# Fused attention and two expert layers on one core: weight staging in eight tiles, expert 1's token rows loaded beside expert 0's, and a PSUM pool of its own for the attention scores

## Chip, cores and metric

The kernel runs on one core of one Trainium2 chip. The metric is device time in microseconds; three runs of the kernel before have a median of 816.23 us (815.91 to 817.96).

## What is computed

Attention with hash buckets feeds a dense feed-forward layer, and that feeds a mixture of eight experts in which every token goes to its best two. The last part is the one that matters here:

```python
top2 = np.argpartition(-noisy_logits, 2, axis=1)[:, :2]
...
for e in range(E):                       # E = 8 experts
    for k in range(2):
        mask = top2[:, k] == e
        h = np.maximum(x[mask] @ w1[e], 0.0)          # 512 -> 1024
        out[mask] += top2_w[mask, k, None] * (h @ w2[e])   # 1024 -> 512
```

There are 1536 tokens of 512 numbers. Every product is made of three fp16 products of high and low parts, so most tiles exist twice (high, low).

## The kernel before, in words

The program has two parts. In the first, a loop over steps `g` (up to 96 attention tiles, `NU` = 96, and a tail of 20 more steps) interleaves attention, the dense layer and the router. Functions are put on a step by `at(g, f, ...)`, and the program is written out in that order; from step 100 on the order on every engine is exactly the written one. In the second part, a list `seq` holds the experts' matrix products, one entry a step `x`: `l1(e, p, f)` makes one block of 128 of the hidden layer for the tokens of part `p` of expert `e`, and `l2(e, p, t)` makes the output of 128 tokens. Experts 1 to 7 have one part of 400 token slots. Expert 0 has two parts, slots 0 to 255 (0,0) and 256 to 399 (0,1), so that its first part can start before the last tokens are routed.

**Order of `seq`.** Eight `l1` of (0,0), its two `l2`; eight `l1` of (0,1), its two `l2`; then expert 1 and so on. The `hold` line puts the first `l1` of the next expert ahead of the `l2` of the last one. At step `x` the program issues first the evictions of step `x-1` (`l1_out` on ACT, L842, then DVE, L843; `l2_out` on ACT, L873, or on ACT and DVE for the short last tile), then the products of step `x`, then what `at` put there.

**Tokens.** The router (`route`) ends for each block of tokens in two scatters to DRAM (`slots`, POOL, L718). `e_load(e, p)` reads an expert's slots back with one transposing DMA to the tile `xg` (L789) and reads the few numbers of weight and address per token to the tile `mt` by small DMAs (L794, L799; where the slots are not a multiple of 128, DVE first writes a default, L797). `e_meta` turns `mt` into weights and addresses on DVE (L809 to L819). `xg` and `mt` have two buffers each. The last block of tokens, chunk (5,1), is routed by the generator `gen` while the `l1` of (0,0) run; its steps are drawn `QX` at a time from step `QS` = 3 on and finished at step `QE`. PE takes part with the transposes `xp` (L578), the logits `pz` (L611, L613) and the running count `pp` (L684, L685), which needs the mask `mk` (DVE, L667).

**Weights.** An expert's weights come in eight blocks of 128 x 1024 fp32 (0 to 3 of `w1`, 4 to 7 of `w2`). `w12_load` brings a block to a staging tile `w32` (L761, L764, on SP's queue), and `w12_split` makes its high part on ACT (L775) and its low part on DVE (L776). There are four staging tiles, so block 4 can be loaded only when block 0 is split.

**Queues.** All of this part's loads are issued by SP, in written order; an entry that waits holds everything behind it. The scatters and the output additions (L880) are issued by POOL.

**PSUM.** Of eight banks, the pool `psr` has one, the pool `psum` seven during attention (two score tiles `s` of two banks, two of tag `h`, one `pv`). When the first part is over, `psum` is closed and `psum2` takes its seven banks: three `ph` for `l1`, three `py` for `l2`, one `xp`. A first tile in a bank of `psum2` waits for the last reader of what lay there. The code behind `tc.If(most > CAP)` (an expert with over 400 tokens) is not entered with these inputs.

Of the kernel before, what the change touches and what calls it, by code (L numbers as in the profile page):

```python
# [8 lines left out]
F32 = mybir.dt.float32  # L9
# [10 lines left out]
DM = H * D  # L20
# [37 lines left out]
PARAM.update(KA={(0, 0, 0): -15, (0, 0, 1): -6, (0, 1, 0): -5, (0, 1, 1): -4, (0, 2, 0): -1, (0, 2, 1): 1, (0, 3, 0): 4, (0, 3, 1): 5, (1, 0, 0): 37, (1, 0, 1): 39, (1, 1, 0): 44, (1, 1, 1): 46, (1, 2, 0): 42, (1, 2, 1): 51, (1, 3, 0): 47, (1, 3, 1): 51}, QA={(0, 0, 0): -15, (0, 0, 1): -3, (0, 0, 2): 1, (0, 0, 3): 3, (0, 1, 0): 8, (0, 1, 1): 9, (0, 1, 2): 17, (0, 1, 3): 21, (0, 2, 0): 24, (0, 2, 1): 28, (0, 2, 2): 30, (0, 2, 3): 33, (1, 0, 0): 37, (1, 0, 1): 41, (1, 0, 2): 47, (1, 0, 3): 52, (1, 1, 0): 57, (1, 1, 1): 56, (1, 1, 2): 60, (1, 1, 3): 69, (1, 2, 0): 72, (1, 2, 1): 69, (1, 2, 2): 80, (1, 2, 3): 84}, VA={(0, 0, 0): -1, (0, 0, 1): -3, (0, 1, 0): -1, (0, 1, 1): -1, (0, 2, 0): 0, (0, 2, 1): 0, (0, 3, 0): -1, (0, 3, 1): -2, (1, 0, 0): -1, (1, 0, 1): -1, (1, 1, 0): 2, (1, 1, 1): -4, (1, 2, 0): -3, (1, 2, 1): -3, (1, 3, 0): 2, (1, 3, 1): -2}, PV={(0, 0, 0): 4, (0, 0, 1): 5, (0, 0, 2): 6, (0, 0, 3): 5, (0, 1, 0): 6, (0, 1, 1): 4, (0, 1, 2): 4, (0, 1, 3): 5, (0, 2, 0): 5, (0, 2, 1): 5, (0, 2, 2): 5, (0, 2, 3): 6, (1, 0, 0): 4, (1, 0, 1): 5, (1, 0, 2): 4, (1, 0, 3): 5, (1, 1, 0): 5, (1, 1, 1): 5, (1, 1, 2): 5, (1, 1, 3): 6, (1, 2, 0): 6, (1, 2, 1): 4, (1, 2, 2): 4, (1, 2, 3): 4}, RA={0: 18, 1: 18, 2: 19, 3: 24, 4: 18}, W=[(g,1) for g in [-6, -4, -3, -1, 0, 0, 1, 1, 2, 4, 4, 7, 8, 8, 9, 10, 11, 12, 13, 14, 15, 16, 16, 17, 18, 20, 20, 22, 22, 23, 23, 24]], EC=lambda g:'AA', LE=lambda nc:nc.sync, HI=lambda g:'AAAA'[g%4], LO=lambda g:[0, 0, 0, 1, 0, 0, 0, 1][g%8]==1, S1=[8, 8, 8, 8, 8, 11, 13, 22], ST={0: 4, 1: 4, 2: 5, 3: 4, 4: 5, 5: 3}, NG=28, WS=lambda i:'PAAA'[i%4], HE=lambda nm,b:'DPDD'[2*(nm=='k')+b], OE=lambda nm,b:'DTDD'[2*(nm=='k')+b], SC=lambda nm,b:'DADD'[2*(nm=='k')+b], R1=2, I0=26, IS=1, O0=56, OS=1, GM=100, BK=3, OH=3, QX=10, QS=3, QE=7, VF=0, T0=12, T1=17, EL=10, WX=5, WL=2, PC=2, GW=2, E0=8, WB=2)  # L58
# [3 lines left out]
def fused(ctx: ExitStack, tc: tile.TileContext, q, k, v, proj, w_in, w_out, w_gate, w_noise, noise,  # L62
# [10 lines left out]
    psum_ctx = ExitStack()  # L73
    psum = psum_ctx.enter_context(tc.tile_pool(name="psum", bufs=2, space=bass.MemoryType.PSUM))
# [173 lines left out]
    def qk(g):  # L248
        b, cc, hp, h, t = where(g)
        qt, kt = qts[b, hp, cc], kts[b, hp]  # L250
        ps = psum.tile([128, 1024], F32, name="s")
# [335 lines left out]
    def route(ci, ta=0, tb=CT):  # L587
# [153 lines left out]
    def r_counts():  # L741
        pc = psum2.tile([128, E], F32, name="pc", tag="py")
# [103 lines left out]
    def l2(e, p, t):  # L846
        py = psum2.tile([128, DM], F32, name="py", bufs=3)
# [132 lines left out]
    for ci in range(B * NCH):  # L980
# [9 lines left out]
        if ci == B * NCH - 2:  # L990
# [63 lines left out]
    psum_ctx.close()  # L1054
# [19 lines left out]
    for e in range(1, E):  # L1074
# [35 lines left out]
    with tc.If(most > CAP):  # L1110
        with tc.tile_pool(name="ov", bufs=1) as ov:
# [8 lines left out]
            hto = ov.tile([128, FE // 128, 2, 128], F16)  # L1120
            yo = ov.tile([128, DM], F32)
            x = ov.tile([128, 1024], F32)
            wt = [wts.tile([128, 2, 4096], F16, name=f"wo{i}", tag="w") for i in range(2)]
            nc.vector.memset(cur, 0.0)
            with tc.For_i(0, E, 1) as e:
# [5 lines left out]
                with tc.If(here > CAP):  # L1131
# [12 lines left out]
                    with tc.For_i(0, (OV + 127) // 128, 1) as k_:  # L1144
                        with tc.If(here > k_ * 128 + CAP):
# [33 lines left out]
                            py = psum2.tile([128, DM], F32, name="pyo", tag="py", bufs=3)  # L1179
# [37 lines left out]
```

## Time and profile before

| what | value |
|---|---|
| median of three runs | 816.23 us (815.91 to 817.96) |
| the profiled execution's own time | 815.95 us |
| its span in the trace | 814.2 us |
| busy share of the span | PE 87%, DVE 66%, ACT 55%, POOL 33% |

The span is what the trace shows from first to last instruction; 1.75 us of the execution's time lie around it. Busy shares are averages: the first 440 us or so (attention) and the experts from 574 us on have different limits, and the stretch between them is where one part hands over to the other.

### The profile page before, as it was taken

Reading aid. Unit: us, or ns where it says so; the run is one execution under the profiler, and the core shown is the slowest. Engines: PE = TensorE matmul, PEld = TensorE weight load, DVE = VectorE, ACT = ScalarE, POOL = GpSimd, SP = SyncE. Lnnn points to the kernel's source line nnn. Section 1 sums busy time; section 2 is a strip of 40 time slices with the busy share of each in tenths; the row PEclk is TensorE's granted clock in tenths of the full one; section 3 lists DMA queues with packets and bytes.
Section 4 is the critical chain, followed back from the end, with each engine's and each line's share of the span. In section 5 each row is a group of like instructions: output and inputs, shape, how many; then the busy total and the mean of one; then the engine's idle time right before and its main releaser. Section 6 shows DMA issues by size and latency. Waiting matters only on the chain.

```text
span 814.2 us, 14902 instructions
## 1 busy us (share of the span) xinstructions
PE 705.3 (87%) x5408; PEld 434.8 (53%) x5409; DVE 541.1 (66%) x1368; ACT 446.9 (55%) x866; POOL 268.0 (33%) x305
## 2 busy tenths in 40 slices
PE   1676578988988798888999999887999999999995
PEld 1343346645754575467567666454545545555452
DVE  8998699996897789569779626673635436354320
ACT  3778768765876586467557525342534435344220
POOL 6444646560444054304212233221121211302113
PEclk9878779999999999999999999998999999999998
DMA  8999689999999999996696650949668768577313
GB/s 219 219 254 218 163 182 195 255 265 237 175 167 211 154 194 194 220 175 106 103 197 115 98 182 17 277 125 196 142 186 226 159 177 198 139 203 156 79 18 44
DMA packets 266942, 139.20 MB, mean 171 GB/s; under 512 B 224176, under 2 KB 242672, under 8 KB 266864
## 3 DMA queue, kind: packets, MB, share of 16 engines
q1 hardware_dynamic: 260848, 125.04, 69.1%
q0 software_dynamic: 6016, 13.16, 8.9%
q8 instruction: 43, 0.70, 0.4%
q14 instruction: 35, 0.29, 0.1%
HBM read 61.48 MB, written 23.20 MB: 104 GB/s over the span
## 4 chain that ended last, share of the span: by engine, by line
PE 43%; DVE 6%; DMA 3%; ACT 2%; issue 1%; POOL 0%; POOLq 0%; ACTq 0%; DVEq 0%
PE ph L832 15%; PE py L863 15%; PE px L472 7%; PE h L461 2%; DMA xg<-slots 2%; DVE er L324 1%; PE py L857 1%; PE pv L369 1%; DMA et<-er 1%; DVE th L491 1%; PE s L255 1%; ACT er L315 1%; DVE e L267 1%; DMA qt<-qsa 0%; POOL out_dram L880 0%
## 5 line engine op out<-in xcount | busy, mean ns | idle before, releaser
L461 PE MATMUL h<-xt,wi 128*128 128x256 f16 x1152 | 141.4, 278 | 7.1 <-DVE th L491 3.9
L832 PE MATMUL ph<-xg,ew 128*128 128x400 f16 (+2 forms) x864 | 136.2, 319 | 7.4 <-DMA xg<-slots 5.3
L776 DVE SCALAR_TENSOR_TENSOR ew<-w,ew 128x1024 f16<-128x1024 f32 x64 | 78.0, 1225 | 83.4 <-ACT ew L775 83.4
L472 PE MATMUL px<-wo,gt 128*128 128x512 f16 x576 | 131.1, 379 | 0.4 <-DVE th L491 0.3
L461 PEld LDWEIGHTS <-wi 128*128 128x128 f16 x1152 | 113.1, 99 | 29.7 <-issue 9.8
L863 PE MATMUL py<-ew,ht 128*128 128x512 f16 x576 | 125.8, 379 | 0.0
L880 POOL DMA_INDIRECT out_dram<-yo,ti x32 | 54.0, 1687 | 211.2 <-ACT yo L873 204.3
L255 PE MATMUL s<-kt,qt 128*128 128x512 f16 (+1 forms) x384 | 87.4, 351 | 35.8 <-DVE mx L267 30.2
L832 PEld LDWEIGHTS <-ew 128*128 128x128 f16 x864 | 81.7, 99 | 59.1 <-issue 9.2
L276 ACT ACTIVATE e<-e,mx 128x768 f32<-128x768 f32 x96 | 89.3, 931 | 28.8 <-DVE mx L267 22.1
L506 POOL TENSOR_TENSOR gt<-th,gt 128x512 f16<-128x512 f32 x48 | 60.5, 1262 | 127.3 <-ACT gt L505 126.9
L267 DVE CUSTOM_DVE_ANT_0 e<-s,zero 128x768 f32<-128x768 f32 x96 | 90.7, 948 | 6.9 <-PE pt L294 3.7
L324 DVE SCALAR_TENSOR_TENSOR er<-e,mx,er 128x768 f16<-128x768 f32 x68 | 72.5, 1069 | 30.1 <-ACT er L315 29.5
L863 PEld LDWEIGHTS <-ht 128*128 128x128 f16 x576 | 56.4, 98 | 67.3 <-issue 0.4
L472 PEld LDWEIGHTS <-gt 128*128 128x128 f16 x576 | 55.1, 98 | 63.0 <-issue 1.3
L315 ACT ACTIVATE er<-e,mx 128x768 f16<-128x768 f32 x68 | 63.1, 930 | 40.1 <-DMA et<-er 26.8
L255 PEld LDWEIGHTS <-qt 128*128 128x128 f16 x384 | 37.2, 103 | 65.0 <-issue 40.1
L842 ACT ACTIVATE ht<-ph 128x400 f16<-128x400 f32 (+2 forms) x72 | 33.4, 465 | 67.7 <-PE ph L832 67.4
L775 ACT ACTIVATE ew<-w 128x1024 f16<-128x1024 f32 x64 | 66.5, 1049 | 7.1 <-DMA w<-in_moe_w_dram 6.9
L873 ACT ACTIVATE yo<-py,wv 128x512 f32<-128x512 f32 x24 | 16.5, 687 | 90.2 <-PE py L863 57.3
L843 DVE SCALAR_TENSOR_TENSOR ht<-ph,ht 128x400 f16<-128x400 f32 (+2 forms) x72 | 37.5, 524 | 36.4 <-ACT ht L842 36.4
L369 PE MATMUL pv<-et,vt 128*64 128x256 f16 x720 | 48.9, 275 | 5.2 <-DMA et<-er 3.2
(234 smaller groups left out, 939.2 us busy)
## 6 DMA issues: line engine op xcount, KB each, us to landing
w<-in_moe_w_dram SPq DMA_DIRECT2D x64, 512.0 KB, 4.7
wraw<-in_moe_w_in_dram SPq DMA_DIRECT2D x16, 512.0 KB, 4.7
wraw<-in_moe_w_out_dram SPq DMA_DIRECT2D x16, 512.0 KB, 4.5
slots<-blank SPq DMA_DIRECT2D x6, 1032.0 KB, 6.8
v<-in_v_dram SPq DMA_DIRECT2D x24, 192.0 KB, 4.3
out_dram<-zeros SPq DMA_DIRECT2D x13, 256.0 KB, 3.4
k<-in_k_dram SPq DMA_DIRECT2D x16, 192.0 KB, 3.6
q<-in_q_dram SPq DMA_DIRECT2D x24, 128.0 KB, 3.3
```

The costliest lines, as they stand in the source:

```text
L255: nc.tensor.matmul(ps[:, n0 * 128:n1 * 128], qt[:, s, h, t, :], kt[:, s, h, n0:n1, :].rearrange("p c t -> p (c t)"), start=(s == 0), stop= ...
L267: nc.vector.tensor_tensor_reduce(e32, st[g]["ps"][:, :S], zero.to_broadcast([128, S]), -0.125, TOP, op0=OP.add, op1=OP.min, accum_out=mx[: ...
L276: nc.scalar.activation(e32, e32, AF.Exp, scale=-1.0, bias=st[g]["mx"][:, 1:2], accum_out=sms[b, cc, hp][:, 2 * h + t:2 * h + t + 1] if g < ...
L315: nc.scalar.activation(er[:, 0], st[g]["e"], AF.Copy, scale=r)
L324: nc.vector.scalar_tensor_tensor(er[:, 1], d["e"], d["mx"][:, 3:4], er[:, 0], op0=OP.mult, op1=OP.subtract)
L461: nc.tensor.matmul(ph[:, a, :], wi[ws][:, d, f0:f0 + 128], xt[:, d, xs, :], start=(d == 0 and ws == 0 and xs == 0), stop=(d == HP - 1 and ...
L472: nc.tensor.matmul(px, gts[ci, f // 2][:, gs, f % 2, t * 128:t * 128 + 128], wo[ws][:, f, :], start=(f == 0 and gs == 0 and ws == 0), stop ...
L506: nc.gpsimd.tensor_tensor(gt[:, 1], th, gt[:, 0], op=OP.subtract)
L775: nc.scalar.activation(hi, x, AF.Copy, scale=SW1 if j == 0 else SW2)
L776: nc.vector.scalar_tensor_tensor(lo, x, SW1 if j == 0 else SW2, hi, op0=OP.mult, op1=OP.subtract)
L832: nc.tensor.matmul(ph[:, :c1 - c0], w[:, ws, d * FE + f * 128:d * FE + f * 128 + 128], xg[e, p][:, xs * HP + d, :], start=(d == 0 and ws = ...
L863: nc.tensor.matmul(py, ht[:, f, hs, t * 128:t * 128 + 128], w[:, ws, f * DM:(f + 1) * DM], start=(i == 0), stop=(i == n - 1))
```

## The change

Eight staging tiles `w32` in place of four. Blocks 4 to 7 of expert 0 are loaded at step `NU + 5`, right behind blocks 0 to 3; blocks 0 to 3 of expert 1 at steps `NU + 12` to `NU + 15`; its blocks 4 to 7 at the start of the second part (x = -3). Splits stay on their steps. `e_load` is divided into the transposing load (`e_load`) and the small ones (`m_load`). Both slot loads, of (0,1) and of expert 1, are put on step `QE`, one after the other, and their small loads behind them; `e_meta` of (0,1) moves from step 8 to step 16, that of expert 1 from step 17 to step 24. In the table of parameters `QX` goes from 10 to 7 and `QE` from 7 to 8. The first `l1` of expert 1 now stands behind the `l2` of (0,1). The scores get a pool `pss` (four banks) that is closed alone; `psum` (tags `h`, `pv`) stays, `psum2` has `ph` and `xp` in the four banks of `pss`, and `l2` uses the two buffers of tag `h`. `pz` of the last chunk and `pc` use `pv`.

```diff
-    psum_ctx = ExitStack()
-    psum = psum_ctx.enter_context(tc.tile_pool(name="psum", bufs=2, space=bass.MemoryType.PSUM))
+    psum = ctx.enter_context(tc.tile_pool(name="psum", bufs=2, space=bass.MemoryType.PSUM))
+    pss_ctx = ExitStack()
+    pss = pss_ctx.enter_context(tc.tile_pool(name="pss", bufs=2, space=bass.MemoryType.PSUM))
...
-        x = m2.tile([128, 1024], F32, name="w32", bufs=4)
+        x = m2.tile([128, 1024], F32, name="w32", bufs=8)
...
         nc.sync.dma_start_transpose(x, slots[r0:r0 + n, :2 * DM])
+
+    def m_load(e, p):
+        c0, c1 = parts(e)[p]
+        n, r0 = c1 - c0, e * CAP + c0
+        nf, nr = n // 128, n % 128
         mt = m2.tile([128, NF + 1, 4], F32, name="mt", bufs=PARAM["XG"])
...
-        py = psum2.tile([128, DM], F32, name="py", bufs=3)
+        py = psum.tile([128, DM], F32, name="py", tag="h")
...
+    for i in range(4):
+        at(NU + 12 + i, w12_load, 1, i)
     for i in range(8):
+        if i >= 4:
+            at(NU + 5, w12_load, 0, i)
         at(NU + 11 + i, w12_split, 0, i)
-        if i < 4:
-            at(NU + 11 + i, w12_load, 0, i + 4)
...
-    psum_ctx.close()
+    pss_ctx.close()
...
-        if n and (p == 0 or n > EA):
+        if n > EA + 1:
             seq.insert(hold, l1s.pop(0))
...
-            at(x - PARAM['WX'], w12_load, e, i)
+            if e > 1 or i >= 4:
+                at(x - PARAM['WX'] if e > 1 else -3, w12_load, e, i)
...
             at(b0, e_load, e, p)
-            at(b0 + 1, e_meta, e, p)
-        else:
-            at(begin[e, p] - PARAM['EL'], e_load, e, p)
-            at(begin[e, p] - 3, e_meta, e, p)
+            at(b0, e_load, EA, 0)
+            at(b0, m_load, e, p)
+            at(begin[e, p] + 6, e_meta, e, p)
+            at(b0 + 1, m_load, EA, 0)
+        else:
+            if e > EA:
+                at(begin[e, p] - PARAM['EL'], e_load, e, p)
+                at(begin[e, p] - PARAM['EL'], m_load, e, p)
+            at(begin[e, p] - (3 if e > EA else -4), e_meta, e, p)
     for x in range(-4, len(seq) + 2):
-        for _ in range(PARAM["QX"]):
+        for _ in range(PARAM["QX"] if x < PARAM["QE"] else 99):
```

SP's queue, from the load of block 4 of expert 1 (`w_6962`) to the end of expert 1's slot load, before; the next two weight loads are blocks 5 and 7:

```order
L764 DMA w_6962<-in_moe_w_dram 128x2x512
L764 DMA w_7061<-in_moe_w_dram 128x2x512
L789 DMA_TRANSPOSE xg<-slots 128x8x144
L794 DMA mt<-slots 128x8
L799 DMA mt<-slots 16x8 x4
L764 DMA w_7134<-in_moe_w_dram 128x2x512
L789 DMA_TRANSPOSE xg<-slots 128x8x400
L794 DMA mt<-slots 128x3x8
L799 DMA mt<-slots 16x8 x4
```

The same place after the change; `w_6865` is block 7 of expert 1, `w_7276` block 0 of expert 2:

```order
L765 DMA w_6865<-in_moe_w_dram 128x2x512
L789 DMA_TRANSPOSE xg<-slots 128x8x144
L789 DMA_TRANSPOSE xg<-slots 128x8x400
L799 DMA mt<-slots 128x8
L804 DMA mt<-slots 16x8 x4
L799 DMA mt<-slots 128x3x8
L804 DMA mt<-slots 16x8 x4
L762 DMA w_7276<-in_moe_w_dram 128x1024
```

Expert 1's slot load (400 wide) has moved ahead of the small loads of (0,1) and of a weight load, and no weight load stands between the blocks of expert 1 and the slot load of (0,1).

DVE, in the middle of the routing of chunk (5,1), before; `rw`, `top`, `ix`, `oh` belong to the router, L843 is an eviction of (0,0), L809 to L815 are `e_meta` of (0,0), and `mk` is what PE's count `pp` waits for:

```order
L843 SCALAR_TENSOR_TENSOR ht<-ph,ht 128x256
L809 TENSOR_SCALAR wv<-mt 128x2
L810 TENSOR_SCALAR wv<-mt 128x2
L811 TENSOR_TENSOR wv<-wv,mt 128x2
L812 TENSOR_TENSOR wv<-wv,mt 128x2
L814 COPY ti<-mt 128x2
L815 TENSOR_TENSOR wv<-wv 128x2
L655 MAX_INDEX ix<-top,rw 128x8
L659 CAST ef<-ix 128x2
L663 TENSOR_TENSOR oh<-iota_e,ef 128x8 x2
L667 TENSOR_TENSOR mk<-oh 128x8
```

The end of that stretch after the change, from the last of the `e_meta` instructions on (line numbers are one to five higher):

```order
L820 TENSOR_TENSOR wv<-wv 128x2
L641 TENSOR_TENSOR rw<-rw 128x8
L643 SCALAR_TENSOR_TENSOR rw<-rw 128x8
L645 SCALAR_TENSOR_TENSOR rw<-z,rw 128x8
L647 TENSOR_TENSOR rw<-rw,noi 128x8
L649 TENSOR_TENSOR rw<-z,rw 128x8
L654 MAX top<-rw 128x8
L656 MAX_INDEX ix<-top,rw 128x8
L848 SCALAR_TENSOR_TENSOR ht<-ph,ht 128x256
L660 CAST ef<-ix 128x2
L664 TENSOR_TENSOR oh<-iota_e,ef 128x8 x2
L668 TENSOR_TENSOR mk<-oh 128x8
```

Six router instructions that stood ahead of the eviction and `e_meta` now stand behind them, and one more eviction stands ahead of `mk`.

PE, where the count `pc` of all tokens (L743) stands, before, at the end of the last `l2` of (0,1):

```order
L857 LDWEIGHTS ht
L857 MATMUL py<-ew,ht 32x256
L743 LDWEIGHTS one
L743 MATMUL pc<-cum,one 128x8
L832 LDWEIGHTS ew
L832 MATMUL ph<-xg,ew 128x400
```

And after, at the same place in PE's order:

```order
L837 MATMUL ph<-xg,ew 128x400
L744 LDWEIGHTS one
L744 MATMUL pc<-cum,one 128x8
L837 LDWEIGHTS ew
L837 MATMUL ph<-xg,ew 128x400
```

The first twelve products of expert 1 (128x400), which stood ahead of both `l2` of (0,1), now stand between them and `pc`. Elsewhere PE's order differs at one place: of the `l1` of (0,0), one more (twelve products of 128x256) stands ahead of `pp`.

## Rows read from the trace of the kernel before

**Rows 1.** The page's first line.

```profile
span 814.2 us, 14902 instructions
```

**Rows 2.** Windows by stage: PE, PEld, DVE, ACT, POOL busy; granted clock; DMA share; GB/s.

```profile
536.40:537.00 0.60, 0.60 (x5) 0.40 (x4) 0.53 (x4) 0.47 (x3) 0.00 (x0) 0.50 0.83 323
574.00:607.00 33.00, 33.00 (x216) 17.39 (x214) 16.61 (x31) 15.02 (x22) 6.63 (x9) 1.00 0.76 195
```

**Rows 3.** Timeline of PE, 520 to 575: start, us, instruction; idle before in brackets.

```profile
524.43 2.78 PE L832 MATMUL ph<-xg,ew 128*128 128x256 f16 x24 [1.54 <-DVE zt L619]
...
529.90 4.14 PE L832 MATMUL ph<-xg,ew 128*128 128x256 f16 x36
536.16 0.18 PE L684 MATMUL pp<-mk,before 128*128 128x8 f16 x1 [2.13 <-DVE mk L667]
...
536.23 4.45 PE L832 MATMUL ph<-xg,ew 128*128 128x256 f16 x24
540.51 10.52 PE L863 MATMUL py<-ew,ht 128*128 128x512 f16 x48
550.87 3.16 PE L832 MATMUL ph<-xg,ew 128*128 128x144 f16 x48
554.59 3.23 PE L832 MATMUL ph<-xg,ew 128*128 128x144 f16 x48 [0.55 <-DVE ht L843]
563.12 4.12 PE L832 MATMUL ph<-xg,ew 128*128 128x400 f16 x12 [5.31 <-DMA xg<-slots]
```

**Rows 4.** The chain that ended last, whole span: start, us, what.

```profile
549.95 13.04 DMA xg<-slots
...
573.96 16.26 PE ph L832 x96
```

**Rows 5.** Timeline of SP's own queue, 480 to 546.

```profile
482.80 1.25 SPq L573 DMA_TRANSPOSE xrt<-xr  x1
...
519.95 1.84 SPq L789 DMA_TRANSPOSE xg<-slots  x1
...
543.33 1.51 SPq L764 DMA_DIRECT2D w<-in_moe_w_dram  x2
544.93 1.95 SPq L789 DMA_TRANSPOSE xg<-slots  x1
```

**Rows 6.** DMA issues at 482.8, 520, 540.5, 544.9, 550, 555.9; us to landing last.

```profile
xrt<-xr SPq DMA_TRANSPOSE x1, 3.1
...
xg<-slots SPq DMA_TRANSPOSE x1, 4.3
...
slots<-xr,si POOLq DMA_INDIRECT x1, 2.8
...
xg<-slots SPq DMA_TRANSPOSE x1, 4.9
...
xg<-slots SPq DMA_TRANSPOSE x1, 13.0
...
mt<-slots SPq DMA_DIRECT2D x1, 6.0 KB, 7.3
```

**Rows 7.** Timeline of DVE, 520 to 570.

```profile
523.64 0.69 DVE L495 SCALAR_TENSOR_TENSOR xr<-px,xr 128x512 f16<-128x512 f32 x1 [2.41 <-ACT xr L486]
...
536.22 0.42 DVE L843 SCALAR_TENSOR_TENSOR ht<-ph,ht 128x256 f16<-128x256 f32 x1
...
538.27 0.17 DVE L713 CAST si<-sf 128x2 int32<-128x2 f32 x1
...
564.09 0.17 DVE L809 TENSOR_SCALAR wv<-mt 128x4 f32<-128x4 f32 x1 [6.37 <-DMA mt<-slots]
```

**Rows 8.** Timeline of POOL, 536 to 545.

```profile
540.47 0.96 POOL L718 DMA_INDIRECT slots<-xr,si  x1 [0.21 <-issue]
```

**Rows 9.** Timeline of ACT, 660 to 664: an output eviction.

```profile
662.10 0.69 ACT L873 ACTIVATE yo<-py,wv 128x512 f32<-128x512 f32 x1 [3.78 <-issue]
```

**Rows 10.** Timeline of PE, 488 to 490.

```profile
489.11 0.25 PE L611 MATMUL pz<-wg,xrt 128*128 128x32 f16 x4
```

More of the change, by code (lines that the diff above doesn't have):

```diff
@@ new lines @@
+PARAM.update(KA={(0, 0, 0): -15, (0, 0, 1): -6, (0, 1, 0): -5, (0, 1, 1): -4, (0, 2, 0): -1, (0, 2, 1): 1, (0, 3, 0): 4, (0, 3, 1): 5, (1, 0, 0): 37, (1, 0, 1): 39, (1, 1, 0): 44, (1, 1, 1): 46, (1, 2, 0): 42, (1, 2, 1): 51, (1, 3, 0): 47, (1, 3, 1): 51}, QA={(0, 0, 0): -15, (0, 0, 1): -3, (0, 0, 2): 1, (0, 0, 3): 3, (0, 1, 0): 8, (0, 1, 1): 9, (0, 1, 2): 17, (0, 1, 3): 21, (0, 2, 0): 24, (0, 2, 1): 28, (0, 2, 2): 30, (0, 2, 3): 33, (1, 0, 0): 37, (1, 0, 1): 41, (1, 0, 2): 47, (1, 0, 3): 52, (1, 1, 0): 57, (1, 1, 1): 56, (1, 1, 2): 60, (1, 1, 3): 69, (1, 2, 0): 72, (1, 2, 1): 69, (1, 2, 2): 80, (1, 2, 3): 84}, VA={(0, 0, 0): -1, (0, 0, 1): -3, (0, 1, 0): -1, (0, 1, 1): -1, (0, 2, 0): 0, (0, 2, 1): 0, (0, 3, 0): -1, (0, 3, 1): -2, (1, 0, 0): -1, (1, 0, 1): -1, (1, 1, 0): 2, (1, 1, 1): -4, (1, 2, 0): -3, (1, 2, 1): -3, (1, 3, 0): 2, (1, 3, 1): -2}, PV={(0, 0, 0): 4, (0, 0, 1): 5, (0, 0, 2): 6, (0, 0, 3): 5, (0, 1, 0): 6, (0, 1, 1): 4, (0, 1, 2): 4, (0, 1, 3): 5, (0, 2, 0): 5, (0, 2, 1): 5, (0, 2, 2): 5, (0, 2, 3): 6, (1, 0, 0): 4, (1, 0, 1): 5, (1, 0, 2): 4, (1, 0, 3): 5, (1, 1, 0): 5, (1, 1, 1): 5, (1, 1, 2): 5, (1, 1, 3): 6, (1, 2, 0): 6, (1, 2, 1): 4, (1, 2, 2): 4, (1, 2, 3): 4}, RA={0: 18, 1: 18, 2: 19, 3: 24, 4: 18}, W=[(g,1) for g in [-6, -4, -3, -1, 0, 0, 1, 1, 2, 4, 4, 7, 8, 8, 9, 10, 11, 12, 13, 14, 15, 16, 16, 17, 18, 20, 20, 22, 22, 23, 23, 24]], EC=lambda g:'AA', LE=lambda nc:nc.sync, HI=lambda g:'AAAA'[g%4], LO=lambda g:[0, 0, 0, 1, 0, 0, 0, 1][g%8]==1, S1=[8, 8, 8, 8, 8, 11, 13, 22], ST={0: 4, 1: 4, 2: 5, 3: 4, 4: 5, 5: 3}, NG=28, WS=lambda i:'PAAA'[i%4], HE=lambda nm,b:'DPDD'[2*(nm=='k')+b], OE=lambda nm,b:'DTDD'[2*(nm=='k')+b], SC=lambda nm,b:'DADD'[2*(nm=='k')+b], R1=2, I0=26, IS=1, O0=56, OS=1, GM=100, BK=3, OH=3, QX=7, QS=3, QE=8, VF=0, T0=12, T1=17, EL=10, WX=5, WL=2, PC=2, GW=2, E0=8, WB=2)
@@ L250, in qk @@
         qt, kt = qts[b, hp, cc], kts[b, hp]
-        ps = psum.tile([128, 1024], F32, name="s")
+        ps = pss.tile([128, 1024], F32, name="s")
         st[g] = {"ps": ps}
@@ L604, in route @@
         if (ci, ta) == LAST:
-            pz = psum2.tile([128, T, 4 * E], F32, name="pz", tag="py")
+            pz = psum.tile([128, T, 4 * E], F32, name="pz", tag="pv", bufs=1)
         else:
@@ L741, in r_counts @@
     def r_counts():
-        pc = psum2.tile([128, E], F32, name="pc", tag="py")
+        pc = psum.tile([128, E], F32, name="pc", tag="pv", bufs=1)
         nc.tensor.matmul(pc, ones, cum[:, 0], start=True, stop=True)
@@ L784, in e_load @@
         n = c1 - c0
-        nf, nr = n // 128, n % 128
         x = m2.tile([128, 2 * HP, n], U16, name="xg", bufs=PARAM["XG"])
@@ L1000, in fused @@
                 at(r0 + 9, e_load, e, 0)
+                at(r0 + 9, m_load, e, 0)
         else:
@@ L1119, in fused @@
             rowt = ov.tile([128, 2 * HP, 128], U16)
-            hto = ov.tile([128, FE // 128, 2, 128], F16)
+            hto = m2.tile([128, FE // 128, 2, 128], F16, name="hto", tag="w32", bufs=8)
             yo = ov.tile([128, DM], F32)
-            x = ov.tile([128, 1024], F32)
+            x = m2.tile([128, 1024], F32, name="xo", tag="w32", bufs=8)
             wt = [wts.tile([128, 2, 4096], F16, name=f"wo{i}", tag="w") for i in range(2)]
@@ L1178, in fused @@
                                                                op1=OP.subtract)
-                            py = psum2.tile([128, DM], F32, name="pyo", tag="py", bufs=3)
+                            py = psum.tile([128, DM], F32, name="pyo", tag="h")
                             for i in range(24):
```

1 line of the change is left out of this document (removed).

## The prediction

> **What bounds the kernel now.** I read the windows by stage first, then the chain of what ended last, then the timelines of PE, SP and DVE in the stretch that stood out. From 574 us on PE works without a gap: one expert's 33 us hold 33.00 us of PE at full clock [rows 2]. Nothing that the change does to staging tiles can shorten that stretch, and since all products remain, only idle PE time can be won. Up to 469 us the written order of all engines is the same in both programs. So the gain lies in the handover, between the last product of the dense layer (522.9) and the first full row of products of expert 1, at 573.96 [rows 4]. There PE stands still three times for over a microsecond: 1.54, 2.13 and 5.31 us [rows 3]. A second cost goes with two of them: behind the 2.13 us the granted clock is 0.50, the lower of its two levels (1.2 GHz) [rows 2], and 24 products take 540.51 - 536.23 = 4.28 us, where 36 alike took 4.14 (0.115 each, 2.76 for 24); behind the 5.31 us, 12 products take 4.12 us [rows 3], where 96 alike take 16.26 (2.03 for 12) [rows 4].
>
> **The first wait (1.54 us): nearly nothing.** The first tile `ph` waits for the bank that the last output of the dense layer leaves when DVE's L495 has read it, at 523.64 + 0.69 = 524.33 [rows 7]. The new pool takes that wait away, since the score banks have long been free. But the tile reads `xg` of (0,0) too, issued at 519.95 [rows 5] and landed 4.3 us later [rows 6], at 524.25; the product starts at 524.43 [rows 3]. Two waits end together, and one stays. The slot load itself waits for scatters that run beside as many weight loads as before. Gain 0 to 1.5 us (if the slots land earlier); I take 0.1 and leave it out of the sum, as nearer to the row of the landing.
>
> **The router's wait (2.13 us).** PE came to `pp` at 536.16 - 2.13 = 534.03 [rows 3]. With 12 more products ahead (12 x 0.115 = 1.4) it comes at 535.4. The mask `mk`, for which it waits, comes later too: in DVE's new order one more eviction stands ahead of it (0.42 us [rows 7]), and six router steps come behind an eviction that waits for ACT. I take 1.0 us later, 537.1, between 0.4 (the one eviction) and 1.5 (three such waits). So PE idles 1.7 instead of 2.13 us, and has 12 products left in place of 24: 1.4 us, or up to 1.5 us more if the clock drops again (1.5 is what the drop cost before, 4.28 - 2.76). No row settles whether it does: an idle of 1.54 us was followed by products of 2.78/24 = 0.116, full speed, one of 2.13 by half speed [rows 3]. The two `l2` of (0,0) then take 10.4 us as before (540.51 to 550.87) [rows 3]. PE is ready for the `l1` of (0,1) at 537.1 + 0.2 + 1.4 + 10.4 = 549.1, or 550.6 with the drop.
>
> **The slots of (0,1).** Their load needs the last scatter. Before, that was issued at 540.47 [rows 8] and landed 2.8 us later [rows 6], at 543.3; but two weight loads stood ahead on SP, the first issued at 543.33, when a staging tile was split, and the slot load went out at 544.93 [rows 5]. Now no weight load waits there. Against it the scatters come later: the mask 1.0 us, and behind it the chain to `si` (to 538.27 [rows 7]) has two evictions in front that need PE's last products, about 1.1 us more. So: second scatter 542.6, landed 545.4, load issued 545.4, half a microsecond later than before. It took 4.9 us beside two weight loads, and a transposing load of similar size 3.1 alone [rows 6]; I take 4.4. Landed 549.8, between 548.5 and 550.3. With PE ready at 549.1 to 550.6, the `l1` of (0,1) start at 550.0, where they started at 550.87: **0.9 us won** (0.2 to 1.7). The 0.55 us wait inside them [rows 3] I leave; it could go (0 to 0.5).
>
> **The slots of expert 1 (5.31 us).** Before, their load was issued at 549.95 and took 13.04 us [rows 4]; PE had been idle since 563.12 - 5.31 = 557.81. Now it goes out right behind that of (0,1), whose issue takes 1.95 us [rows 5]: 547.4. Its other condition, that PE be done with the `xg` of (0,0), is met at about 539. Even if it takes 13.0 us again it lands at 560.4. It is needed later than before: the `l1` of (0,1) end at 550.0 + 6.94 = 556.9 (550.87 to 557.81 before), and both `l2` of (0,1), which took from 567.24 (563.12 + 4.12) to 573.96, 6.7 us with `pc`, now stand ahead of it: 563.6. A margin of 3 us even then: **5.3 us won**. And with no idle there the twelve products take 2.03 in place of 4.12: **2.1 us won**.
>
> **Edits at nothing.** Blocks 4 to 7 of expert 0, 2 MB, now load from 471 us on behind the first four. Their cover is PE's dense layer; behind them on SP stands the transposed load L573, issued at 482.80 [rows 5] and landed 3.1 us later [rows 6], at 485.9, read by PE at 489.11 [rows 10]. 3.2 us of delay are free, each further one would be paid. The splits keep their order and no longer wait for loads. The four blocks of expert 1 next to them only take the slot on SP that blocks 4 to 7 of expert 0 had. `e_meta` of expert 1 leaves a place where it held DVE for 6.37 us, to 564.09 [rows 7], with one eviction of (0,1) behind it; that of (0,1) gets a like place (first rival). Two output banks in place of three: last rival.
>
> **The sum.** 0.9 + 5.3 + 2.1 = 8.3 us. Against the profiled execution: its span of 814.2 [rows 1] becomes 805.9, its own 815.95 becomes 807.65. The median of the runs is 0.28 above that execution, so **807.9 us**. Its own range: 805.3 (slots of (0,0) a microsecond earlier, no drop, the 0.55 gone) to 810 (drop, slots of (0,1) late, a short new wait).
>
> **Rivals.**
>
> *The wait moves to the small loads.* The `mt` of (0,1) is now issued behind expert 1's slot load, and `e_meta` of (0,1) stands on DVE ahead of the last two evictions of (0,1). Before, an `mt` issued behind such a load landed after 7.3 us [rows 6], about with the slots, and DVE went on at 564.09 [rows 7], 1.1 us after the slots of expert 1 had landed (562.99). If those land at 560.4, DVE starts at 561.5, is through its eight small steps at 562.4 and has eviction 6 at 562.8. The `l2` of (0,1) reads it with its 21st of 24 products, 20 x 0.22 = 4.4 us after 556.9, at 561.3: 1.5 us lost, and up to 3 if the load takes longer than 13 us or the clock drops behind it: 809.4 to 811. For it speaks the order on SP; against it, that the load now goes out with no weight load beside it. The Trainium skill ("DMA: Bandwidth & Descriptors", section "Queues, rings and completion order") says that each DMA engine takes a ring's descriptors in order. By that rule the small loads cannot overtake the slots, and the 7.3 us agree.
>
> *No change.* Expert 1's slots would have to land at 563.6 + 7 = 571 or later, 23 us after issue, against 13.0 measured; or weight loads of expert 2, which queue behind them, come as late as that. About 815 us.
>
> *More is won.* The slots of (0,0) land a microsecond or more earlier, since one weight load fewer runs beside the last scatters, and all that follows moves with them: 1.5 us of the first wait, with the clock held: 805 or a little under.
>
> *Slower.* `l2` turns over two banks in place of three. An eviction (0.69 us on ACT [rows 9]) must be over before the bank's next tile, which starts one `l2` tile later, 10.52/2 = 5.26 us [rows 3]. If ACT, in its order, is held for over 5.26 us by a split that waits for a load, PE waits, in all experts. With a bubble of 0.9 us behind each of 24 tiles, as a single bank would give, it costs 21 us: about 829. The price decides from some 0.45 us a tile on. The rows speak against it, 0.69 to 5.26. The Trainium skill ("Perfetto Trace Analysis", sections "Optimization Strategy" and "Matmul Optimizations") warns of this: a gap that repeats on the busy engine can mean too few buffers, and all eight banks should be used. By that rule the change takes a bank from the very tiles that bound the kernel; the rows here show no repeated gap and leave room.
>
> **How the numbers follow.** Forecast 0.72; the small loads 0.12; more won 0.08; no change 0.05; slower 0.03. The range takes the forecast with its bounds and most of the first rival, 805.2 to 811.3. A measurement of this kernel tells about 0.3% (2.4 us) from no change. Faster by over that (below 813.8): 0.72 + 0.12 + 0.08, less a little for a long first rival, 0.91; within 0.3%: 0.05; slower: 0.04.
>
> **What would show it.** In the changed kernel's timeline of PE the first `ph` still waits, now for `xg`; the wait at `pp` is between 1 and 2.5 us; the `l1` of expert 1 have no wait for `xg` and run at full clock (0.17 us a product); SP issues the 400-wide slot load within 2 us of the 144-wide one; experts 2 to 7 keep PE without a gap, as in [rows 2]. Wrong would be: a new wait over 2 us in the `l2` of (0,1) behind DVE, a wait for the slots of (0,1) of over 1.5 us, L573's reader waiting at 489, or gaps between the `l2` tiles of experts 2 to 7.

## The result, and the profile after

The changed kernel takes 810.71 us, median of 7 runs (806.07 to 812.06); the kernel before 817.61 us, median of 7 (815.91 to 820.92). The ratio is 0.9906, with a 95% interval of 0.988 to 0.9933: 0.94%, or 7.7 us of 817.6, won. (The ratio goes by all runs; the two medians by themselves lie 6.9 us apart.) The forecast was 807.9 us in a range of 805.2 to 811.3.

The profiled execution of the changed kernel took 812.06 us; its span, 810.4 us, is 3.8 us under that of [rows 1]. That is less than the change brought in the stretch it touches, because the attention part, the same in both up to 469 us, came 2.29 us later in this execution. It was 2.28 us late already at 455 us (the same product starts at 457.62 and at 455.34), where both programs still have the same order. So from here on the handover is measured by itself: from the first router product `pz` of the last chunk to the first 400-wide product behind the count `pc`. For the kernel before, these are two rows of PE's timeline that were not shown yet (start, duration, instruction):

```profile
522.54 0.26 PE L611 MATMUL pz<-wg,xrt 128*128 128x32 f16 x4
...
573.82 16.40 PE L832 MATMUL ph<-xg,ew 128*128 128x400 f16 x96
```

That is 573.82 - 522.54 = 51.28 us. The same timeline of the changed kernel (its line numbers are one to five higher), to be read against [rows 3]:

```profile
524.83 0.25 PE L612 MATMUL pz<-wg,xrt 128*128 128x32 f16 x4
...
525.97 2.78 PE L837 MATMUL ph<-xg,ew 128*128 128x256 f16 x24 [0.79 <-DMA xg<-slots]
...
538.18 0.18 PE L685 MATMUL pp<-mk,before 128*128 128x8 f16 x1 [1.02 <-DVE mk L668]
...
538.24 1.47 PE L837 MATMUL ph<-xg,ew 128*128 128x256 f16 x12
539.55 10.52 PE L868 MATMUL py<-ew,ht 128*128 128x512 f16 x48
552.99 6.18 PE L837 MATMUL ph<-xg,ew 128*128 128x144 f16 x72 [2.92 <-DMA xg<-slots]
559.72 1.66 PE L837 MATMUL ph<-xg,ew 128*128 128x144 f16 x24 [0.55 <-DVE ht L848]
561.22 5.34 PE L868 MATMUL py<-ew,ht 128*128 128x512 f16 x24
...
567.92 2.20 PE L837 MATMUL ph<-xg,ew 128*128 128x400 f16 x12
...
569.99 16.40 PE L837 MATMUL ph<-xg,ew 128*128 128x400 f16 x96
```

The handover takes 569.99 - 524.83 = 45.16 us: 6.1 us won. The wait of 5.31 us for expert 1's slots is gone, and the twelve products behind it take 2.20 in place of 4.12 us. But a wait that was not there before has come: 2.92 us for the slots of (0,1). The windows around it (busy PE, PEld, DVE, ACT, POOL, then granted clock, DMA share, GB/s) show what follows:

```profile
552.00:553.00 1.00, 0.01 (x1) 0.01 (x1) 0.00 (x0) 0.00 (x0) 0.70 (x2) 0.89 1.22 217
553.00:556.00 3.00, 3.00 (x26) 3.00 (x26) 0.42 (x2) 1.24 (x2) 0.00 (x0) 0.50 1.25 268
556.00:557.00 1.00, 1.00 (x17) 1.00 (x15) 1.00 (x1) 0.33 (x2) 0.00 (x0) 0.90 0.54 65
...
578.00:611.00 33.00, 33.00 (x216) 17.39 (x215) 16.02 (x34) 14.20 (x20) 7.08 (x8) 1.00 0.72 181
```

PE works from 553 on, but at a granted clock of 0.50 (1.2 GHz, the lower level) until 556. The `l1` of (0,1) take 561.22 - 552.99 = 8.23 us, where they took 6.94. The last row answers to the second of [rows 2]: 33.00 us busy of 33, as before. What led to the wait is in the chain (start, us, what), on POOL and on DVE:

```profile
543.50 3.96 DMA slots<-xr,si
547.48 5.47 DMA xg<-slots
552.99 3.94 PE ph L837 x36
```

```profile
541.67 1.52 POOL L719 DMA_INDIRECT slots<-xr,si  x1 [4.34 <-ACT ew L776]
...
543.50 1.97 POOL L719 DMA_INDIRECT slots<-xr,si  x1 [0.22 <-issue]
```

```profile
540.73 0.17 DVE L714 CAST si<-sf 128x2 int32<-128x2 f32 x1
...
541.14 5.76 DVE L777 SCALAR_TENSOR_TENSOR ew<-w,ew 128x1024 f16<-128x1024 f32 x5
```

Each of the last two scatters took 0.96 us to issue before (the first at 539.21; the second in [rows 8]); now they take 1.52 and 1.97, and the last lands 3.96 us after issue in place of 2.8 [rows 6]. Of the 1.2 us more to the landing, 1.0 is the longer issue. They stand beside five splits of expert 1's weights on DVE. SP's own queue, against [rows 5]:

```profile
547.48 6.22 SPq L789 DMA_TRANSPOSE xg<-slots  x2
553.75 0.59 SPq L799 DMA_DIRECT2D mt<-slots  x1
...
558.68 3.10 SPq L762 DMA_DIRECT2D w<-in_moe_w_dram  x4
```

Both slot loads go out one behind the other, the first as soon as the last scatter has landed, with no weight load ahead of it.

### The profile page after: what moved, and what is told of

It reads as the page before. It is cut to its first block, busy times and chain, and to the rows that moved or that the text cites. A ratio compares the mean times of both kernels' runs of the same rounds, so it can differ in the third digit from the quotient of the medians.

```text
span 810.4 us, 14910 instructions
## 1 busy us (share of the span) xinstructions
PE 703.6 (87%) x5408; PEld 435.3 (54%) x5409; DVE 539.5 (67%) x1368; ACT 446.6 (55%) x866; POOL 271.1 (33%) x305
## 4 chain that ended last, share of the span: by engine, by line
PE 41%; DVE 5%; DMA 4%; ACT 2%; issue 1%; POOL 1%; POOLq 0%; ACTq 0%; DVEq 0%
PE ph L837 15%; PE py L868 14%; PE px L473 6%; PE h L462 3%; DMA et<-er 2%; PE py L862 1%; PE pv L370 1%; PE s L256 1%; DVE th L492 1%; DVE er L325 1%; DMA xg<-slots 1%; DMA slots<-xr,si 0%; ACT er L316 0%; ACT gt L506 0%; DMA qt<-qsb 0%
## 5 line engine op out<-in xcount | busy, mean ns | idle before, releaser
L837 PE MATMUL ph<-xg,ew 128*128 128x400 f16 (+2 forms) x864 | 133.9, 317 | 4.3 <-DMA xg<-slots 3.7
```

What stands on the lines that cost most here:

```text
L837: nc.tensor.matmul(ph[:, :c1 - c0], w[:, ws, d * FE + f * 128:d * FE + f * 128 + 128], xg[e, p][:, xs * HP + d, :], start=(d == 0 and ws = ...
```

## The experiments

The reasons on trial were these. **Theory:** the staging tiles and the order of the slot loads bring the gain, the PSUM part nearly nothing; and the new wait comes from the scatters, which the splits beside them slow. **Rivals:** the PSUM banks bring it; the place next to the other slot load is what counts, or costs; the scatters are slow for another reason. The measure is the handover of each profile, since the dense layer's end (the start of `pz`) lay anywhere from 519.47 to 525.82 us in these programs.

| kernel | first `pz` | first 400-wide behind `pc` | handover, us | wait for slots (0,0) or its bank | wait for slots (0,1) |
|---|---|---|---|---|---|
| before | 522.54 | 573.82 | 51.28 | 1.54 | 0 |
| changed | 524.83 | 569.99 | 45.16 | 0.79 | 2.92 |
| psum_only | 522.73 | 576.14 | 53.41 | 1.70 | 0.49 |
| stage_only | 525.82 | 570.55 | 44.73 | 1.50 | 2.68 |
| slots_back | 524.09 | 567.28 | 43.19 | 0.47 | 2.40 |
| four_tiles | 521.34 | 570.34 | 49.00 | 2.15 | 5.18 |
| hold_back | 525.48 | 571.38 | 45.90 | 1.74 | 2.91 |
| split_late | 522.57 | 563.62 | 41.05 | 0.71 | 0 |
| split_late_t | 524.52 | 565.62 | 41.10 | 0.73 | 0.31 |
| lo_late | 525.03 | 570.06 | 45.03 | 1.17 | 2.89 |
| lo_later | 523.26 | 573.04 | 49.78 | 1.70 | 0.82 |
| stage_split | 519.47 | 560.93 | 41.46 | 1.50 | 0 |
| split_back | 521.51 | 563.34 | 41.83 | 1.89 | 0 |

Each row is one execution. How far single profiles can be trusted shows in rows of nearly the same order: the changed kernel, stage_only, hold_back and lo_late lie between 44.73 and 45.90, and one kernel profiled twice (split_late, split_late_t) gave 41.05 and 41.10. Of the kernel before there is one profile. For the router's mask PE waits 2.13 us in the two rows without the router's new order (before, psum_only) and 1.01 or 1.02 in all others; the new order (`QX`, `QE`, the places of `e_meta`) was not tried by itself.

**1. The PSUM part alone** (in the kernel before):

```
-    psum_ctx = ExitStack()
-    psum = psum_ctx.enter_context(tc.tile_pool(name="psum", bufs=2, ...))
+    psum = ctx.enter_context(tc.tile_pool(name="psum", bufs=2, ...))
+    pss_ctx = ExitStack()
+    pss = pss_ctx.enter_context(tc.tile_pool(name="pss", bufs=2, ...))
...
-        py = psum2.tile([128, DM], F32, name="py", bufs=3)
+        py = psum.tile([128, DM], F32, name="py", tag="h")
...
```

> Only the PSUM pools of the change, in the kernel before: the scores get a pool of their own, the outputs of the experts take the banks of the dense layer, two in place of three. The measure here and below is the handover: from the first router product of the last chunk to the first 400-wide product of expert 1 behind the count; before it took 51.28 us, after 45.16. Theory (the staging tiles and the slots' order bring the gain, the banks nearly nothing): the handover takes 50.5 to 51.3 us, the wait of PE for the slots of expert 1 is still over 4.5 us. Rival (the banks bring it): 46 to 48 us.

Measured: a handover of 53.41 us; the whole kernel took 819.81 us against 821.91, one run each. The rival falls, but a handover 2.1 us longer than before was not expected, and the wait for expert 1's slots, 3.92 us, is under the 4.5 that the theory named. PE's timeline, then POOL's, DVE's and the scatter's landing (last number, us):

```profile
536.53 0.18 PE L685 MATMUL pp<-mk,before 128*128 128x8 f16 x1 [2.13 <-DVE oh L664]
...
536.60 2.78 PE L833 MATMUL ph<-xg,ew 128*128 128x256 f16 x24
...
554.99 0.98 PE L833 MATMUL ph<-xg,ew 128*128 128x144 f16 x12 [2.35 <-DVE ht L844]
...
565.69 3.87 PE L833 MATMUL ph<-xg,ew 128*128 128x400 f16 x12 [3.92 <-DMA xg<-slots]
```

```profile
540.84 1.99 POOL L719 DMA_INDIRECT slots<-xr,si  x1 [0.21 <-issue]
```

```profile
540.78 4.63 DVE L777 SCALAR_TENSOR_TENSOR ew<-w,ew 128x1024 f16<-128x1024 f32 x4 [0.52 <-ACT ew L776]
```

```profile
slots<-xr,si POOLq DMA_INDIRECT x1, 6.1
```

After the same wait of 2.13 us for the mask the clock held here, and 24 products took 2.78 us in place of 4.45 [rows 3]. So the evictions came earlier, and with them the splits: at 540.78, beside the second scatter, which took 1.99 us. In the kernel before, the half clock had kept the splits back until the scatters were issued:

```profile
542.07 4.63 DVE L776 SCALAR_TENSOR_TENSOR ew<-w,ew 128x1024 f16<-128x1024 f32 x4 [0.52 <-ACT ew L775]
```

The earlier splits also let weight loads go out on SP (at 542.03) while that scatter was under way; it landed after 6.1 us, 4.1 after the end of its issue, where it is 2.0 in the changed kernel. Everything behind it came late, and what PE won at the mask was lost again at the slots. That the clock held at this place because of the PSUM pools is not shown: with one profile of each kernel, it may as well differ from one execution of the kernel before to the next.

**2. All but the PSUM part**, that is, in the changed kernel:

```
-        py = psum.tile([128, DM], F32, name="py", tag="h")
+        py = psum2.tile([128, DM], F32, name="py", bufs=3)
```

and the other lines of experiment 1 the other way round.

> The changed kernel with the PSUM pools of before (three output banks, the first tile of the experts waits for the dense layer's last eviction again), all else as changed. Theory: the handover takes 45 to 46.2 us, at most a microsecond more than the changed kernel's 45.16, and the first product of the experts waits as long as now, since the slots of (0,0) land about with the eviction. Rival (the banks bring the gain): 48 to 51 us.

Measured: 44.73 us, 0.3 under what the theory gave as its least, with the new wait at 2.68 us. One part of the theory fails: the first product waited 1.50 us, for the eviction of the dense layer, and not about as long as in the changed kernel (0.79). So the gain needs no more than the staging and the order; two output banks or three make no difference that shows.

**3. Expert 1's slot load back at its own step:**

```
             at(b0, e_load, e, p)
-            at(b0, e_load, EA, 0)
             at(b0, m_load, e, p)
             at(begin[e, p] + 6, e_meta, e, p)
-            at(b0 + 1, m_load, EA, 0)
...
-            if e > EA:
-                at(begin[e, p] - PARAM['EL'], e_load, e, p)
-                at(begin[e, p] - PARAM['EL'], m_load, e, p)
...
+            at(begin[e, p] - PARAM['EL'], e_load, e, p)
+            at(begin[e, p] - PARAM['EL'], m_load, e, p)
```

> The changed kernel with expert 1's slot load back at its own later step, behind the small loads of (0,1); the eight staging tiles stay. Theory A (SP held by weight loads was what made it late; with eight tiles nothing stands ahead of it): the load goes out 2 to 4 us later than now and still lands before PE needs it, no wait for it, the handover takes 44.2 to 45.5 us, and the slots of (0,1) land 0 to 1 us sooner, since no second load runs beside them. Theory B (the place next to the other slot load is the gain): PE waits 4 us or more for expert 1's slots, the handover takes 49 us or more.

SP's own queue, PE's timeline, and the window behind PE's wait (columns as above):

```profile
546.57 1.28 SPq L789 DMA_TRANSPOSE xg<-slots  x1
...
550.45 3.39 SPq L789 DMA_TRANSPOSE xg<-slots  x1
```

```profile
551.74 3.16 PE L837 MATMUL ph<-xg,ew 128*128 128x144 f16 x48 [2.40 <-DMA xg<-slots]
...
565.21 2.20 PE L837 MATMUL ph<-xg,ew 128*128 128x400 f16 x12
```

```profile
552.00:553.00 1.00, 1.00 (x20) 1.00 (x18) 0.00 (x0) 0.32 (x2) 0.00 (x0) 1.00 1.15 234
```

Theory B falls: the load goes out 3.9 us behind the other, and PE never waits for it. At 43.19 us the handover is even 2.0 us shorter than the changed kernel's, and 1.0 under the least of theory A. Behind a wait of 2.40 us the clock held, and the `l1` of (0,1) took 558.51 - 551.74 = 6.77 us in place of 8.23; they also started 0.5 us earlier after `pz`. The slots of (0,1) landed at most 551.74 - 546.57 = 5.17 us after issue, where they took 5.5 with the other load behind them. So no more than 0.3 us of the landing can be laid to the second load; 1.5 of the 2.0 us are the clock, and why it held here and not behind the 2.92 us is not shown.

**4. Four staging tiles again, the new order kept:**

```
-        x = m2.tile([128, 1024], F32, name="w32", bufs=8)
+        x = m2.tile([128, 1024], F32, name="w32", bufs=4)
...
-    for i in range(4):
-        at(NU + 12 + i, w12_load, 1, i)
     for i in range(8):
-        if i >= 4:
-            at(NU + 5, w12_load, 0, i)
         at(NU + 11 + i, w12_split, 0, i)
+        if i < 4:
+            at(NU + 11 + i, w12_load, 0, i + 4)
...
-            if e > 1 or i >= 4:
-                at(x - PARAM['WX'] if e > 1 else -3, w12_load, e, i)
+            at(x - PARAM['WX'], w12_load, e, i)
...
```

> The changed kernel with four staging tiles again, and the weight loads where they stood before; the new order of the slot loads, of the small loads and of the router, and the PSUM pools, stay. Theory A (it is the order of the slot loads that counts: expert 1's stands right behind that of (0,1), and only two weight loads are held ahead of both): expert 1's slots land before PE needs them, no wait over 0.5 us for them, the handover takes 44 to 47 us. Theory B (without the four further tiles SP is held until splits free tiles, and both slot loads go out late): the first slot load over 1.5 us later than the landing of the last scatter, a wait for the slots of (0,1) of over 4 us, handover 48 us or more.

SP's own queue, the landing of the last scatter (us, last), and PE's timeline:

```profile
539.93 2.64 SPq L765 DMA_DIRECT2D w<-in_moe_w_dram  x3
547.72 8.40 SPq L789 DMA_TRANSPOSE xg<-slots  x2
```

```profile
slots<-xr,si POOLq DMA_INDIRECT x1, 6.7
```

```profile
552.79 6.89 PE L837 MATMUL ph<-xg,ew 128*128 128x144 f16 x72 [5.18 <-DMA xg<-slots]
...
568.27 2.21 PE L837 MATMUL ph<-xg,ew 128*128 128x400 f16 x12
```

The numbers are theory B's: 49.00 us, a wait of 5.18 us. Its reason is not, and one point is theory A's: PE has no wait for expert 1's slots. The slot load went out the moment the scatter had landed, so SP was not held. The landing itself took 6.7 us, beside three weight loads that the splits let go at 539.93. Without the further tiles, 2.3 of the 6.1 us are left. Of the 3.8 us that they bring, 2.7 are the landing of the last scatter (6.66 against 3.96); that scatter also goes out 1.0 us later after `pz` (19.71 against 18.67), behind a first wait of 2.15 us in place of 0.79. What the tiles do here is to have the weight loads done before the last scatters.

**5. The first tile of expert 1 ahead of the `l2` of (0,1) again:**

```
-        if n > EA + 1:
+        if n and (p == 0 or n > EA):
             seq.insert(hold, l1s.pop(0))
```

> The changed kernel with the first l1 tile of expert 1 ahead of the l2 of (0,1) again, so that nothing but the l1 of (0,1) covers expert 1's slots. In the changed kernel these landed at about 557, the l1 of (0,1) ended at 561.2. Theory (the slots come early enough without the cover of the l2): PE waits less than 0.5 us for expert 1's slots, the handover takes 44.5 to 46 us. Rival (the cover is needed): a wait of 1 to 4 us there, with the lower clock behind it, handover 47 us or more.

PE's timeline at the place where the slots of expert 1 are first needed:

```profile
561.11 3.69 PE L837 MATMUL ph<-xg,ew 128*128 128x144 f16 x36 [0.55 <-DVE ht L848]
```

These 36 products are 24 of (0,1) and, without a gap, 12 of expert 1. The slots were there; the cover of the two `l2` was not needed. Of the 0.74 us that the handover is longer than the changed kernel's, more than all, 0.95, is in the first wait (1.74 against 0.79).

**6. The first five splits of expert 1 one step later:**

```
-PARAM.update(... S1=[8, 8, 8, 8, 8, 11, 13, 22], ...)
+PARAM.update(... S1=[9, 9, 9, 9, 9, 11, 13, 22], ...)
```

> The changed kernel with the first five splits of expert 1's weights one step later (9 in place of 8), behind the output of the first 128 rows, so that VectorE does no 128x1024 split while GpSimd issues the last two scatters. Theory (the splits beside them slow the scatters): each scatter takes about 0.96 us as before, in place of 1.52 and 1.97; the slot load of (0,1) goes out 1.5 to 2.5 us earlier after the router's first product, the wait of 2.92 us falls below 1.2 us, the granted clock stays at full speed behind it, and the handover takes 41.5 to 43.5 us. Rival (the scatters are slow for another reason, or the late splits hold up the evictions of (0,1)): scatters over 1.4 us, handover 44.5 us or more.

The timelines of POOL, DVE and PE:

```profile
539.42 0.96 POOL L719 DMA_INDIRECT slots<-xr,si  x1 [4.35 <-issue]
540.68 0.96 POOL L719 DMA_INDIRECT slots<-xr,si  x1 [0.23 <-issue]
```

```profile
544.34 5.77 DVE L777 SCALAR_TENSOR_TENSOR ew<-w,ew 128x1024 f16<-128x1024 f32 x5 [5.29 <-ACT ew L776]
```

```profile
547.77 2.41 PE L837 MATMUL ph<-xg,ew 128*128 128x144 f16 x36
```

The scatters take 0.96 us each, land in 2.8, and the `l1` of (0,1) have no wait for slots left; their clock is at 1.00. The handover takes 41.05 us, a little under the expected least. Timed:

> The kernel with the first five splits of expert 1 at step 9, timed. Its handover took 41.05 us against 45.16 in the changed kernel and 51.28 before. Theory: the 4.1 us come on top of the change's own gain of some 7.7 us: a ratio to the kernel before of 0.983 to 0.988 (804 to 808 us where before takes 818). Rival (some of it is taken back, or the profiled execution was a lucky one): a ratio of 0.989 to 0.993, as the changed kernel's own.

Measured: 809.13 us, median of 6, against 819.19 (11 runs): ratio 0.9871, interval 0.9848 to 0.9894. Its profile gives a handover of 41.10 us, 10.2 under that of before, or 1.25% of its time: the ratio agrees. The interval overlaps that of the changed kernel (0.988 to 0.9933), and the two were not timed side by side, so that this version beats it rests on the handovers, not on the times.

**7. Only DVE's half of these splits moved.** The split is cut into two functions, `w12_hi` (ScalarE) and `w12_lo` (DVE), and the second goes first to the next step:

```
-            at(x, w12_split, e, i)
+            if e == 1 and x == 8:
+                at(x, w12_hi, e, i)
+                at(x + 1, w12_lo, e, i)
+            else:
+                at(x, w12_split, e, i)
```

> Of expert 1's first five splits only VectorE's half (the low part, a two-input 128x1024 operation) is moved one step later, behind the output of the first 128 rows; ScalarE's half (the high part) stays beside the scatters. With both halves moved the two scatters took 0.96 us each, landed 2.8 us after issue, and the handover took 41.05 us. Theory A (VectorE's half is what slows the scatters): 0.96 us each again, handover 40.5 to 42 us. Theory B (ScalarE's half, or both reading the staging tiles, slows them): at least one scatter takes over 1.3 us, handover 43 us or more.

DVE's timeline, the five low parts:

```profile
541.47 5.76 DVE L791 SCALAR_TENSOR_TENSOR ew<-w,ew 128x1024 f16<-128x1024 f32 x5
```

This told nothing apart. On DVE nothing stands between the two steps, so its half still ran beside the scatters, at 541.47; these took 1.59 and 1.96 us, and the handover 45.03. With `at(x + 3, w12_lo, e, i)` it stands behind an eviction that needs PE:

> As the kernel that moved only VectorE's half of the first five splits, but three steps later (11), behind the first eviction of (0,1), since one step later nothing stood ahead of it on VectorE and it ran beside the scatters as before. ScalarE's half stays beside them. Theory A (VectorE's half slows the scatters): 0.96 us each, landed about 2.8 us after issue; the first l1 product of (0,1) waits less than 1 us for the slots, though evictions behind the late splits may wait up to 5 us. Theory B (ScalarE's half is enough to slow them): a scatter of over 1.3 us and a wait for the slots of over 2 us.

The timelines of POOL, of ACT and DVE (the high and the low parts), and of PE:

```profile
540.69 0.96 POOL L719 DMA_INDIRECT slots<-xr,si  x1 [4.33 <-ACT ew L786]
541.96 0.96 POOL L719 DMA_INDIRECT slots<-xr,si  x1 [0.22 <-issue]
```

```profile
539.05 4.83 ACT L786 ACTIVATE ew<-w 128x1024 f16<-128x1024 f32 x5
...
551.41 5.76 DVE L791 SCALAR_TENSOR_TENSOR ew<-w,ew 128x1024 f16<-128x1024 f32 x5
```

```profile
549.91 3.16 PE L851 MATMUL ph<-xg,ew 128*128 128x144 f16 x48 [0.82 <-DMA xg<-slots]
558.57 5.86 PE L851 MATMUL ph<-xg,ew 128*128 128x144 f16 x48 [5.50 <-DVE ht L862]
```

Theory A: with ScalarE's half still beside them the scatters are fast again. The wait of 5.50 us is the price for splits in front of evictions (up to 5 us were foreseen); with it the handover takes 49.78 us, so this is a test and no improvement.

**8. The late splits with other parts undone.** With the PSUM pools of before (the edits of 6 and 2):

> The kernel with the late splits, with the PSUM pools of before. Theory (the PSUM part brings nothing in the handover): 40.5 to 42.2 us, as with the new pools (41.05 and 41.10). Rival (three output banks and the wait for the dense layer's last eviction cost something once the slots come early): 42.5 us or more.

Measured: 41.46 us, of which 1.50 is the first wait; the theory holds. (The whole kernel took 803.00 us in its one run, the least of all; its `pz` came 3.1 us earlier than in experiment 6, at 519.47, so the time says nothing on the handover.) And with expert 1's slot load at its own step (the edits of 6 and 3):

> Late splits and expert 1's slot load at its own later step together. The scatters are then fast and no second load runs beside that of (0,1). Theory (each of the two already takes the wait away; what is left are the waits for the router and for the slots of (0,0)): handover 40.5 to 41.3 us, a ratio to the kernel before of 0.984 to 0.989, no better than the late splits alone. Rival (the two add up): 39.5 us or less. Third case (behind the small loads expert 1's slots now come too late): a wait for them, handover over 42 us.

Measured: 41.83 us; 805.98 us, median of 4, against 817.46 (7 runs), ratio 0.9868, interval 0.9834 to 0.9901. The handover is 0.5 longer than expected, and the first wait, 1.89 us against 0.71 with the late splits alone, is more than that. The two gains do not add to each other.

## Why the prediction was right, and where its sizes were off

**The slots of expert 1, 5.3 + 2.1 = 7.4 us: as forecast.** From the end of the `l1` of (0,1) to the end of the handover it took 573.82 - 557.81 = 16.01 us before and 569.99 - 561.22 = 8.77 now: 7.24 won. The load went out next to the other and landed after 8.2 us, in place of 13.0, at about 557; it was needed at 567.9, so the margin was 11 us, where 3 had been taken. What experiments 3 and 4 add is that either part takes this wait away by itself: the further tiles with the load at its old step, or the place next to the other load with four tiles. What the further tiles do beyond that is to keep weight loads away from the last scatters.

**The step that was mis-sized is the slots of (0,1).** It was to win 0.9 us; it won 0.17, and 1.29 went to the half clock behind the new wait: 0.17 - 1.29 + 7.24 = 6.1, for 8.3. Put on the clock of the profile of before (2.29 less), the row of terms reads:

- The mask was taken as 1.0 us later. By this clock it was not later: PE waited 1.02 us for it, not 1.7, the clock held, and PE was ready for the `l1` at 550.07 - 2.29 = 547.8, not at 549.1 or after. In part that is the first wait, 0.75 us shorter: counted from the experts' first product, `pp` came 0.48 us later than before (12.21 against 11.73), at the lower end of the 0.4 to 1.5 named.
- The second scatter went out at 541.2 (forecast 542.6), but landed 3.96 us later, where the 2.8 of [rows 6] was taken over. The load was therefore issued at 545.2; forecast 545.4. That these agree is luck: one error of 1.4 us and one of 1.2 cancel.
- The slots landed 5.5 us after that, beyond the 4.9 that was the upper bound of the 4.4 taken.

The forecast called a wait of over 1.5 us for the slots of (0,1) wrong, and it is 2.92. The duration of the scatter came from rows in which nothing ran beside it on DVE. The order of the changed kernel puts five splits there, and experiments 6 and 7 show that these make the scatter late. Without them the term is worth far more than forecast: in experiment 6 the `l1` of (0,1) start 547.77 - 522.57 = 25.20 us after `pz`, 3.1 earlier than the 550.87 - 522.54 = 28.33 of before. Against the changed kernel it is 3.0: the first scatter goes out 16.8 us after `pz` in both, from there to the last landing it is 4.1 us in place of 5.8, and the slot load accounts for the other 1.3 us.

Here the Trainium skill ("SBUF — State Buffer", section "Who interferes with whom") bears on it: an instruction of VectorE with two inputs in SBUF contends with one of GpSimd that reads SBUF, and the later one waits. The low part of a split reads the staged block and the high part, both in SBUF, and the rows agree: 0.96 us alone, 1.52 and 1.97 beside it, and no effect of ScalarE's half. The same section reports DMAs that another two-input operation did not hold up; for this scatter the rows decide.

**The first wait** went from 1.54 to 0.79 us and ends with the slots, as said. With the changed order it was 0.47 to 2.15 us from one profile to the next, so this 0.75 is nothing to count on.

**Edits at nothing** held: neither the transposed load's reader, at 491.39, nor the experts waited, and two output banks show no cost (experiments 2 and 8). With the PSUM part alone the handover took 2.1 us longer, by a way that the text had not considered: early splits and weight loads beside a scatter. Whether the pools set that off stays open.

**The rivals.** The small loads did not hold DVE: `e_meta` of (0,1) came at 560.02 with no wait. No repeated gap came in the experts. The time itself lies in the range, 0.6 us under its upper end and 2.8 us over the forecast; of this, 1.4 us lie in the median of before, 816.23 over the 3 runs that the forecast was made from and 817.61 over all 7.

What stays open: why the slots of (0,1) landed 5.5 us after issue here and at most 4.2 us in experiment 6 (547.77 - 543.54); in the other kernels with fast scatters it was 3.1 to 4.7. A scatter-add to the output, 2.50 us to issue in the one and 1.62 in the other, runs beside both; that it is the cause was not tried. Open too is what the router's new order is worth by itself.

## What to carry to other kernels

When a change lets an engine run earlier, ask what bulk work becomes ready with it, and what it will stand beside: here weight splits came to lie beside two small scatters on the path that sets the end. A duration taken over from a trace holds only with the same neighbours; list what runs on the other engines in the row it comes from. And where the rest of the kernel varies by more than the effect, measure the stage between two of its own instructions. Here rows of nearly the same order agreed within 1.2 us, against differences of 6.1 and 10.2; a second profile of the kernel before would have told how far its own 51.28 us vary.

## What the runs showed of the hardware

- An indirect scatter's issue on GpSimd takes 0.96 us alone or beside ScalarE's half of the splits, and 1.52 to 1.99 beside VectorE's 128x1024 half, in seven kernels. A scatter-add to the output takes 2.50 us in the changed kernel, where the splits were running when it began, and 1.62 in experiment 6, where they began after it.
- Counted from the end of its issue, each of the last two scatters lands after 1.7 to 2.2 us, alone as beside the splits; the last took 4.1 and 4.7 us where weight loads went out beside it as well (experiments 1 and 4). That is not the whole of it: in the changed kernel the two scatters of the block of tokens before took 3.3 and 2.7 us with neither beside them, and why is not known.
- The length of an idle stretch did not settle whether the clock drops. After 2.13 us it fell to 0.50 in the kernel before [rows 2] and stayed at 1.00 in experiment 1, as it did after 2.40 us in experiment 3; after 2.68 us (experiment 2) and 2.92 us it fell. The window behind the 2.13 us of experiment 1:

```profile
536.60:539.20 2.60, 2.60 (x26) 2.34 (x27) 2.43 (x17) 0.93 (x4) 0.00 (x0) 1.00 0.30 108
```
